# Four integer adds of a weight conversion on GpSimd instead of VectorE, with new tables for the order of block 0, the middle and the stores

## The chip, the cores and the metric

The kernel runs on one core of a Trainium2 chip. Its engines work side by side, each through its own list of instructions in order, and wait for one another by semaphores: TensorE (PE; its weight loads are listed as PEld), VectorE (DVE), ScalarE (ACT), GpSimd (POOL), and SyncE (SP), which here issues the DMA transfers. The metric is the device time of one launch in microseconds (us).

## The reference

Attention in chunks of 64 tokens, and on its output a feed-forward layer with a gate. Cut to what is computed:

```python
batch, n_heads, seq, head_dim = 8, 8, 576, 64              # float32
chunk = 64; scale = 1.0 / np.sqrt(64)
scores = scale * np.matmul(q_c, k_c.transpose(0, 1, 2, 4, 3))   # per chunk of 64
scores = scores - np.max(scores, axis=-1, keepdims=True)
attn = np.exp(scores)
attn = attn / (np.sum(attn, axis=-1, keepdims=True) + 1e-09)
out = np.matmul(attn, v_c)
x = out.transpose(0, 2, 1, 3).reshape(4608, 512)
h = x @ w_in                    # 512 x 2048
g = h * np.clip(h + 3.0, 0.0, 6.0) / 6.0
return g @ w_out                # 2048 x 512
```

## The kernel before

The 4608 tokens are worked on in 9 blocks of 512. A block goes through attention (two parts of four heads each), a first product with w_in, the gate, and a second product with w_out. An fp32 product is made of three matmuls of 128x512 in a shorter format: high by high (L364), high by low (L365), low by high (L366). So every operand has a high half, cast by ScalarE, and a low half, the rest, subtracted by VectorE.

Block 0 is done in plain form, and while it runs the weights are brought in. They come as 64-bit words and are converted tile by tile; tile ft (0 to 15) holds 128 columns of w_in and 128 rows of w_out. Tiles 0 to 3 are converted in halves i (w_in) and o (w_out). The order is written out by hand in the table FIRST, one token for a step, a letter and the tile:

- W load (L152), H high words (ScalarE, L161), L low words (ScalarE, L165), P shift (VectorE, L168), A add of the low bits (VectorE, L171), C cast to the high half (ScalarE, L179), D the low half (VectorE, L187), U store of the converted words (L182, L184), X store of a quarter of the tile for later use (L421). H, P and A work on a scratch tile u, L on a scratch tile r (uh and rh for halves).
- M the first product of block 0 with a tile, N the second; between them the gate: R (ScalarE, L553), G (VectorE, L555), K (ScalarE, L558), B (VectorE, L560).
- A0 and A1 with a small letter or S, Q, V, T: attention of block 1, its two parts. Q and V load; S scores (TensorE, L240); m, u, e, z, x softmax (VectorE, but e on ScalarE); t swap, c place; v multiply (TensorE, L330), h copy of its result (ScalarE, L351), l its low half (VectorE, L352).
- S0, T0 and so on without A: attention of block 0. I: matmuls that fill time.

The tokens are recorded in this order; so on every engine the instructions stand in the order of the tokens that use it, an engine that has to wait holds all that stands behind it, and SP's transfers are issued in token order too. The M and N products use two banks of PSUM called h in turn, and the multiply of block 1's attention uses these two as well: its results are out of them when L352 has run.

Behind block 0 comes the middle (first products of blocks 1 and 2), and then three pairs of blocks, which are done with seven products instead of eight. Their weights are sums of quarters. prepare() makes them: a load of words or an add on VectorE, four adds on GpSimd (L454), a cast on ScalarE (L457), a low half on VectorE (L460), a store to DRAM (L463). The sums and the kept quarters are read back as streams into tiles ws. Tables give the due times, counted in products: MID for the attention of later blocks in the middle, OUT_SUMS and IN_SUMS for the sums, STORES for quarters that are kept in the middle. In the pairs, L481 and L482 make the high and low halves of the operands.

Of the kernel before, what the change touches and what calls it, by code (L numbers as in the profile page):

```python
# [52 lines left out]
FIRST = """
Q0 S0a S0b I0 T0 m0a m0b Q1 W0i u0a u0b S01 I2 S10 I1 m01 e00 u01 z00 e01 S11 I1 T1 m10 H0i W1i V0 z01 W2i L0i m11 x00 W0o x01 L1i W4 P0i n10 I1 e10 z10 V1 H1i
W1o A0i n11 e11 z11 t00 t01 I2 W3i c00 v00 c01 A0Q x10 L2i L0o W5 v01 I2 h00 C0i h01 x11 t10 t11 I0 P1i c10 A1i C1i D0i c11 M0.00 H4 M0.02 H0o l00 l01 M1.00 v10
v11 M1.01 D1i M1.02 M0.01 P4 P0o H2i P2i A2i h10 h11 M1.10 M1.12 A0o l10 l11 L4 M0.12 C0o W3o M0.10 M0.11 M1.11 A4 C2i L1o R0 A0S D2i G0 M2 D0o C4 H3i P3i L3i
D4 K0 B0 N0 A3i A0T H5 W8 R1 G1 H1o C3i K1 D3i M3 P1o P5 A1o L5 B1 R2 G2 L3o C1o W6 D1o H6 M4 A5 P6 R3 G3 U4 C5 D5 W2o K2 B2 L6 N1 H2o L2o H3o M5 A6 P2o W9 A2o
P3o R4 W12 C2o G4 D2o K3 B3 A0m A3o L8 K4 C6 U5 R5 W7 D6 U6 H7 P7 C3o D3o L7 B4 A1Q G5 H8 N2 M6 A7 C7 R6 X4o N3 W13 P8 W10 K5 A8 D7 G6 B5 N4 C8 A0u U7 U8 D8 W11
L9 K6 H10 A0e B6 M7 P10 N5 H9 R7 A0z L10 P9 A0V W14 G7 A9 C9 A0x U9 N6 L11 M8 A0t D9 A10 K7 A0c0 A0c1 A0c2 M9 C10 B7 D10 R8 N7 G8 R9 G9 A0c3 K8 K9 B9 U10 X10o
H11 B8 A1T P11 H12 M10 R10 A11 P12 A0c4 C11 N8 G10 W15 A0v D11 A1S L12 U11 X11i A0h K10 N8e A0l A12 M11 A2Q N9 C12 L13 D12 R11 U12 X8o B10 X0i N10 H13 M12 A1m  # L60
P13 G11 A13 L14 C13 A1u X7i A1e K11 D13 R12 A1z A1x H14 P14 X12i M13 R13 B11 A1V G12 A1t G13 X1o N11 A1c U13 K12 A14 B12 C14 X3o X2o K13 D14 H15 N11e X0o A1v
A1h U14 P15 X5i A1l L15 X5o A15 N12 B13 M14 N13 C15 R14 G14 D15 K14 M15 R15 X3i X7o B14 G15 X14i U15 A2S K15 B15 X13o X15o
""".split()
# [907 lines left out]
```

## Time and profile before

| | us |
|---|---|
| median of 3 runs (lowest, highest) | 774.25 (774.15, 775.13) |
| the profiled execution | 774.06 |
| its span in the trace | 772.2 |
| TensorE busy | 765.9 |
| TensorE weight loads busy | 631.0 |
| VectorE busy | 620.7 |
| ScalarE busy | 409.2 |
| GpSimd busy | 149.4 |

The span is what the trace covers; the time of the execution has 1.86 us around it. TensorE ran at the full clock in all but the last slice of the page's table. Busy times of engines overlap, so they don't add up to the span; what counts is the time in which TensorE waits, and for whom.

### The profile page before, as it was taken

Reading aid. Unit: us, or ns where it says so; the run is one execution under the profiler, and the core shown is the slowest. Engines: PE = TensorE matmul, PEld = TensorE weight load, DVE = VectorE, ACT = ScalarE, POOL = GpSimd, SP = SyncE. Lnnn points to the kernel's source line nnn. Section 1 sums busy time; section 2 is a strip of 40 time slices with the busy share of each in tenths; the row PEclk is TensorE's granted clock in tenths of the full one; section 3 lists DMA queues with packets and bytes.
Section 4 is the critical chain, followed back from the end, with each engine's and each line's share of the span. In section 5 each row is a group of like instructions: output and inputs, shape, how many; then the busy total and the mean of one; then the engine's idle time right before and its main releaser. Section 6 shows DMA issues by size and latency. Waiting matters only on the chain.

```text
span 772.2 us, 13644 instructions
## 1 busy us (share of the span) xinstructions
PE 765.9 (99%) x5551; PEld 631.0 (82%) x5551; DVE 620.7 (80%) x749; ACT 409.2 (53%) x551; POOL 149.4 (19%) x134
## 2 busy tenths in 40 slices
PE   8999999999999999999999999999999999999998
PEld 6788888888888788888888888888888888888887
DVE  6998867888799888787899876778998756669960
ACT  5998646465664534545666434354837333346330
POOL 0000012465561143322300002221100012221000
PEclk9999999999999999999999999999999999999999
DMA  9996898898877798975676777666656775565573
GB/s 363 408 344 234 300 331 306 305 329 293 320 246 248 287 325 300 338 269 187 243 273 238 246 218 256 236 213 223 232 198 219 225 221 191 197 207 200 194 238 113
DMA packets 51838, 199.07 MB, mean 258 GB/s; under 512 B 4672, under 2 KB 10816, under 8 KB 38720
## 3 DMA queue, kind: packets, MB, share of 16 engines
q1 hardware_dynamic: 51488, 197.94, 72.9%
q8 instruction: 44, 0.72, 0.4%
q10 hardware_dynamic: 288, 0.26, 0.1%
q14 instruction: 18, 0.15, 0.1%
HBM read 153.62 MB, written 44.56 MB: 257 GB/s over the span
## 4 chain that ended last, share of the span: by engine, by line
PE 93%; DMA 3%; DVE 2%; ACT 1%; issue 1%; POOL 0%; SPq 0%; ACTq 0%; DVEq 0%; POOLq 0%
PE acc L364 23%; PE acc L365 22%; PE acc L366 22%; PE h L364 7%; PE h L366 7%; PE h L365 7%; PE h L330 2%; PE two L235 2%; DMA a<-hl 1%; DMA hl<-words 1%; PE two L240 1%; DMA qk<-qk_in 1%; POOL hl L454 0%; PE two L309 0%; DVE xop L482 0%
## 5 line engine op out<-in xcount | busy, mean ns | idle before, releaser
L364 PE MATMUL acc<-xop,ws 128*128 128x512 f32 (+1 forms) x616 | 239.6, 389 | 0.0
L365 PE MATMUL acc<-xop,ws 128*128 128x512 f32 (+1 forms) x616 | 239.0, 388 | 0.6 <-DVE xop L482 0.6
L366 PE MATMUL acc<-xop,ws 128*128 128x512 f32 (+1 forms) x616 | 238.8, 388 | 0.0
L365 PEld LDWEIGHTS acc<-xop,ws 128*128 128x128 f32 x616 | 115.7, 188 | 24.6 <-DVE xop L482 1.0
L364 PEld LDWEIGHTS acc<-xop,ws 128*128 128x128 f32 x616 | 115.6, 188 | 23.9
L366 PEld LDWEIGHTS acc<-xop,ws 128*128 128x128 f32 x616 | 115.7, 188 | 23.7
L482 DVE TENSOR_TENSOR xop<-g,xop 128x1024 fp32r<-128x1024 f32 x96 | 117.6, 1257 | 6.8 <-ACT xop L481 6.8
L481 ACT CAST xop<-g 128x1024 fp32r<-128x1024 f32 x96 | 96.9, 1052 | 31.7 <-PE acc L366 22.4
L664 ACT ACTIVATE r<-acc,half 128x512 f32<-128x512 f32 x100 | 66.9, 686 | 68.6 <-DVE acc L631 54.6
L665 DVE SCALAR_TENSOR_TENSOR g<-r,acc 128x512 f32<-128x512 f32 x100 | 66.7, 681 | 41.9 <-ACT r L664 39.2
L454 POOL TENSOR_TENSOR hl<-hl 128x256 f32<-128x256 f32 x64 | 58.4, 915 | 208.5 <-DVE hl L440 111.9
L750 POOL TENSOR_TENSOR g<-g 128x512 f32<-128x512 f32 x24 | 31.0, 1293 | 325.6 <-DVE g L665 325.6
L364 PE MATMUL h<-xop,ws 128*128 128x512 f32 (+1 forms) x176 | 67.8, 385 | 0.0
L366 PE MATMUL h<-xop,ws 128*128 128x512 f32 (+1 forms) x176 | 67.6, 384 | 0.0
L365 PE MATMUL h<-xop,ws 128*128 128x512 f32 (+1 forms) x176 | 67.6, 384 | 0.0
L664 ACT ACTIVATE r<-h,half 128x512 f32<-128x512 f32 x28 | 19.3, 689 | 85.4 <-DVE h L631 83.3
L631 DVE TENSOR_TENSOR u<-h,p 128x512 f32<-128x512 f32 x32 | 22.1, 689 | 32.2 <-PE h L366 25.4
L364 PE MATMUL acc<-x,w 128*128 128x512 f32 x112 | 44.2, 395 | 0.0
L366 PE MATMUL acc<-x,w 128*128 128x512 f32 x112 | 43.6, 390 | 0.0
L365 PE MATMUL acc<-x,w 128*128 128x512 f32 x112 | 43.6, 390 | 0.0
L263 ACT ACTIVATE e<-e 128x1024 f32<-128x1024 f32 (+1 forms) x18 | 18.2, 1013 | 47.8 <-DVE e L261 47.8
L364 PEld LDWEIGHTS h<-xop,ws 128*128 128x128 f32 x176 | 33.1, 188 | 6.6
(120 smaller groups left out, 1217.3 us busy)
## 6 DMA issues: line engine op xcount, KB each, us to landing
ws<-b SPq DMA_DIRECT2D x56, 1024.0 KB, 4.9
ws<-a SPq DMA_DIRECT2D x24, 1024.0 KB, 5.3
ws<-a SPq DMA_DIRECT2D x24, 768.0 KB, 4.4
qk<-qk_in SPq DMA_DIRECT2D x16, 1024.0 KB, 7.7
w<-w_in_out SPq DMA_DIRECT2D x12, 1024.0 KB, 11.6
v<-v_in SPq DMA_DIRECT2D x17, 512.0 KB, 5.9
out_t<-o SPq DMA_DIRECT2D x30, 256.0 KB, 5.9
b<-hl SPq DMA_DIRECT2D x12, 512.0 KB, 5.4
```

Source lines behind the costliest of these rows:

```text
L235: PE.matmul(t[to, a, g, :], lhsT=self.qk[rows, i, 0, c, o], rhs=self.qk[rows, i, 1, c, o], start=True, stop=True)
L263: ACT.activation(out=flat(self.e), in_=src if self.by_product else flat(self.e), func=AF.Exp, scale=SCALE)
L364: PE.matmul(ps, lhsT=a_h, rhs=b_h, start=first, stop=False, skip_group_check=more)
L365: PE.matmul(ps, lhsT=a_h, rhs=b_l, start=False, stop=False, skip_group_check=more)
L366: PE.matmul(ps, lhsT=a_l, rhs=b_h, start=False, stop=last, skip_group_check=more)
L454: POOL.tensor_tensor(out=to, in0=x, in1=y, op=op)
L481: ACT.copy(out=t[:, :, 0], in_=src)
L482: DVE.tensor_tensor(out=t[:, :, 1], in0=src, in1=t[:, :, 0].bitcast(F32), op=ALU.subtract)
L631: return lambda: DVE.tensor_tensor(out=out, in0=x, in1=y, op=ALU.add)
L664: return (lambda: ACT.activation(out=r, in_=ps, func=AF.Relu, bias=half, scale=1.0 / 6.0), lambda: DVE.scalar_tensor_tensor(out=out, in0=r ...
L665: lambda: DVE.scalar_tensor_tensor(out=out, in0=r, scalar=1.0, in1=ps, op0=ALU.min, op1=ALU.mult))
L750: sub = lambda o, x, y: lambda: POOL.tensor_tensor(out=o, in0=x, in1=y, op=ALU.subtract)
```

## The change

The add of the low bits to the converted words goes to GpSimd for four tiles: the whole tiles 15, 6 and 7, and the first half of tile 2. On VectorE it is an instruction of uint16 operands (listed as L171, 128x2048, or 128x1024 for a half); on GpSimd it is an add of int32 words (128x1024, or 128x512). Beside that five tables have new numbers or a new order: FIRST, MID, OUT_SUMS, STORES and IN_SUMS. Tokens that move in FIRST are, among others: A0Q (a load of 1 MB) ahead of W3i; D2i ahead of A0S; A5 ahead of C1o and D1o; X4i (a store) ahead of the loads W9, W12 and W7; U6 behind A1Q; L9 three ScalarE steps later; A0v (multiply) behind A1S (scores); A0V, a load, later. Some stores of quarters go from the middle into FIRST, and STORES has 12 entries for 14.

```diff
-W1o A0i n11 e11 z11 t00 t01 I2 W3i c00 v00 c01 A0Q x10 L2i L0o W5 v01 I2 h00 C0i h01 x11 t10 t11 I0 P1i c10 A1i C1i D0i c11 M0.00 H4 M0.02 H0o l00 l01 M1.00 v10
+W1o A0i n11 e11 z11 t00 t01 A0Q I2 W3i c00 v00 c01 x10 L2i L0o W5 v01 I2 h00 C0i h01 x11 t10 t11 I0 P1i c10 A1i C1i D0i c11 M0.00 H4 M0.02 H0o l00 l01 M1.00 v10
...
-D4 K0 B0 N0 A3i A0T H5 W8 R1 G1 H1o C3i K1 D3i M3 P1o P5 A1o L5 B1 R2 G2 L3o C1o W6 D1o H6 M4 A5 P6 R3 G3 U4 C5 D5 W2o K2 B2 L6 N1 H2o L2o H3o M5 A6 P2o W9 A2o
+D4 K0 B0 N0 A3i A0T H5 W8 R1 G1 H1o C3i K1 D3i M3 P1o P5 A1o L5 B1 R2 G2 L3o A5 C1o W6 D1o H6 P6 M4 R3 G3 U4 C5 W2o K2 X4i D5 B2 L6 N1 H2o L2o H3o M5 A6 P2o W9
...
-STORES = (('X4i', -120), ('X6i', -120), ('X12o', -118.7), ('X9i', -117.2), ('X9o', -113.7), ('X10i', -112), ('X11o', -101.5), ('X8i', -101.3), ('X6o', -99.8), ('X15i', -99), ('X14o', -96.8), ('X13i', -93.1), ('X1i', -89.0), ('X2i', -89))
+STORES = (('X12o', -118.7), ('X10i', -116), ('X11i', -114.7), ('X4o', -112.5), ('X11o', -104.5), ('X9o', -101.7), ('X15i', -99), ('X13i', -93.1), ('X2i', -91), ('X6o', -89.8), ('X1i', -88), ('X14i', -70.4))
+ADDED = ((15, None), (2, 0), (6, None), (7, None))
...
         def add(self):
-            DVE.tensor_tensor(out=self.u, in0=self.u, in1=self.r, op=ALU.add)
+            (POOL if (self.ft, self.m) in ADDED else DVE).tensor_tensor(out=self.u, in0=self.u, in1=self.r, op=ALU.add)
```

Lines of the changed kernel are higher by one from L67 on. GpSimd's list, from its first instructions to the sums of the middle (hl are sums, g operands of a pair), before:

```order
masks.py:199 ISA
masks.py:199 AFFINE_SELECT ident<-ident 128x128
L454 TENSOR_TENSOR hl<-hl 128x256 x20
L685 TENSOR_TENSOR g<-g 128x512 x5
L454 TENSOR_TENSOR hl<-hl 128x256 x4
L685 TENSOR_TENSOR g<-g 128x512
L454 TENSOR_TENSOR hl<-hl 128x256 x4
L685 TENSOR_TENSOR g<-g 128x512 x2
```

and now:

```order
masks.py:199 ISA
masks.py:199 AFFINE_SELECT ident<-ident 128x128
L172 TENSOR_TENSOR uh<-uh,rh 128x512
L172 TENSOR_TENSOR u<-u,r 128x1024 x3
L455 TENSOR_TENSOR hl<-hl 128x256 x20
L686 TENSOR_TENSOR g<-g 128x512 x4
L455 TENSOR_TENSOR hl<-hl 128x256 x4
L686 TENSOR_TENSOR g<-g 128x512 x2
```

The four adds stand first, ahead of all sums; behind them sums and operand adds change places a little.

VectorE's list in block 0, from the conversions of tiles 1 and 5 to those of 2o, 3o and 6 (an ISA row with u or uh is the add; w_1_615 and w_641 are the tiles 1o and 5; w_1_692 is 2o), before:

```order
L187 TENSOR_TENSOR w_1_615<-uh,w_1_615 128x2x256
L171 ISA u<-u,r 128x2048
L168 TENSOR_SCALAR u<-u 128x1024
L555 SCALAR_TENSOR_TENSOR r<-r,h 128x512
L187 TENSOR_TENSOR w_641<-u,w_641 128x4x256
L560 TENSOR_TENSOR g<-r,g 128x512
L171 ISA u<-u,r 128x2048
L168 TENSOR_SCALAR uh<-uh 128x512
L171 ISA uh<-uh,rh 128x1024
L168 TENSOR_SCALAR uh<-uh 128x512
L555 SCALAR_TENSOR_TENSOR r<-r,h 128x512
L187 TENSOR_TENSOR w_1_692<-uh,w_1_692 128x2x256
```

and now (w_1_616, w_641, w_1_691 are the same tiles):

```order
L172 ISA u<-u,r 128x2048
L188 TENSOR_TENSOR w_1_616<-uh,w_1_616 128x2x256
L169 TENSOR_SCALAR u<-u 128x1024
L556 SCALAR_TENSOR_TENSOR r<-r,h 128x512
L188 TENSOR_TENSOR w_641<-u,w_641 128x4x256
L561 TENSOR_TENSOR g<-r,g 128x512
L169 TENSOR_SCALAR uh<-uh 128x512
L172 ISA uh<-uh,rh 128x1024
L169 TENSOR_SCALAR uh<-uh 128x512
L556 SCALAR_TENSOR_TENSOR r<-r,h 128x512
L188 TENSOR_TENSOR w_1_691<-uh,w_1_691 128x2x256
```

The add of tile 5 (first ISA row) stands ahead of the low half of tile 1o, and the add of tile 6, which stood behind the row L560 ahead of the shift of 2o, is gone from this engine.

TensorE's list where tile 11 follows tile 10 (h<-x are first products, acc<-g second ones; w_794 is tile 8, w_963 tile 11), before:

```order
L366 MATMUL acc<-g,w_794 128x512
L330 MATMUL h<-e,v 64x64 x32
L240 MATMUL two<-qk 64x64 x32
L364 MATMUL acc<-g,w_794 128x512
L365 MATMUL acc<-g,w_794 128x512
L366 MATMUL acc<-g,w_794 128x512
L364 MATMUL h<-x,w_963 128x512
L365 MATMUL h<-x,w_963 128x512
```

and now (w_793, w_966):

```order
L367 MATMUL acc<-g,w_793 128x512
L241 MATMUL two<-qk 64x64 x32
L331 MATMUL h<-e,v 64x64 x32
L365 MATMUL acc<-g,w_793 128x512
L366 MATMUL acc<-g,w_793 128x512
L367 MATMUL acc<-g,w_793 128x512
L365 MATMUL h<-x,w_966 128x512
L366 MATMUL h<-x,w_966 128x512
```

The multiply (L330, now L331) and the scores (L240, now L241) have changed places; the rest of TensorE's list is the same from end to end.

## Rows read from the trace of the kernel before

**Rows 1.** The page, part 1: busy time, share of the span, instructions

```profile
PE 765.9 (99%) x5551; PEld 631.0 (82%) x5551; DVE 620.7 (80%) x749; ACT 409.2 (53%) x551; POOL 149.4 (19%) x134
```

**Rows 2.** TensorE's waits: line <- releaser: us in total, times, longest

```profile
PE acc L365 <- DVE xop L482: 0.6, 1, 0.6
PE h L364 <- DVE r L555: 0.3, 1, 0.3
```

**Rows 3.** Timeline of TensorE: start us, us, engine, line, operation, out<-in, count

```profile
46.72 0.39 PE L364 MATMUL h<-x,w 128*128 128x512 f32 x1
46.94 0.39 PE L365 MATMUL h<-x,w 128*128 128x512 f32 x1
47.29 0.50 PE L366 MATMUL h<-x,w 128*128 128x512 f32 x1
...
66.47 0.40 PE L366 MATMUL h<-x,w 128*128 128x512 f32 x1
...
77.30 1.11 PE L240 MATMUL two<-qk 64*64 64x64 f32 x64
78.34 0.50 PE L364 MATMUL acc<-g,w 128*128 128x512 f32 x1
...
79.23 0.50 PE L364 MATMUL h<-x,w 128*128 128x512 f32 x1
```

**Rows 4.** Timeline of VectorE, 39 to 66 us

```profile
39.24 0.68 DVE L560 TENSOR_TENSOR g<-r,g 128x512 fp32r<-128x512 f32 x1
39.84 1.22 DVE L171 CUSTOM_DVE_ANT_0 u<-u,r 128x2048 uint16<-128x2048 uint16 x1
40.98 0.42 DVE L168 TENSOR_SCALAR uh<-uh 128x512 int32<-128x512 int32 x1
41.53 0.69 DVE L171 CUSTOM_DVE_ANT_0 uh<-uh,rh 128x1024 uint16<-128x1024 uint16 x1
...
46.02 1.22 DVE L187 TENSOR_TENSOR w<-u,w 128x1024 fp32r<-128x1024 f32 x1
...
48.77 0.68 DVE L560 TENSOR_TENSOR g<-r,g 128x512 fp32r<-128x512 f32 x1
...
51.11 0.68 DVE L168 TENSOR_SCALAR u<-u 128x1024 int32<-128x1024 int32 x1
...
65.09 1.20 DVE L187 TENSOR_TENSOR w<-u,w 128x1024 fp32r<-128x1024 f32 x1
```

**Rows 5.** Windows, 41.5 to 66.3: us; PE, PEld, DVE, ACT, POOL busy (instructions); clock; DMA

```profile
41.50:66.30 24.80, 24.80 (x110) 20.19 (x108) 24.30 (x32) 21.11 (x26) 0.00 (x0) 1.00 0.81 299
```

**Rows 6.** The page, part 5: GpSimd's adds of L750: busy us, mean ns

```profile
L750 POOL TENSOR_TENSOR g<-g 128x512 f32<-128x512 f32 x24 | 31.0, 1293 | 325.6 <-DVE g L665 325.6
```

**Rows 7.** Timeline of GpSimd

```profile
154.96 2.55 POOL L685 TENSOR_TENSOR g<-g 128x512 f32<-128x512 f32 x2 [1.81 <-DVE g L665]
...
255.21 3.19 POOL L454 TENSOR_TENSOR hl<-hl 128x256 f32<-128x256 f32 x4 [19.55 <-DMA hl<-words]
...
277.26 4.44 POOL L454 TENSOR_TENSOR hl<-hl 128x256 f32<-128x256 f32 x1 [18.87 <-DMA hl<-words]
...
545.37 2.15 POOL L750 TENSOR_TENSOR t<-g 128x512 f32<-128x512 f32 x1
```

**Rows 8.** Timeline of VectorE beside two of those adds

```profile
156.82 0.71 DVE L269 TENSOR_SCALAR z<-z 128x16 f32<-128x16 f32 x1
...
545.03 1.35 DVE L482 TENSOR_TENSOR xop<-g,xop 128x1024 fp32r<-128x1024 f32 x1 [0.24 <-ACT xop L481]
```

**Rows 9.** Line 269: duration ns least/median/longest, first and last start

```profile
L269 DVE TENSOR_SCALAR z<-z x18: 174/175/714, 11.2 to 573.9; 128x16 f32<-128x16 f32 x18
```

**Rows 10.** Timeline of ScalarE

```profile
46.41 1.12 ACT L161 ACTIVATE u<-w 128x1024 f32<-128x1024 f32 x1
...
77.87 1.07 ACT L351 CAST x<-h 128x512 fp32r<-128x512 f32 x2
```

**Rows 11.** DMA issues at 37 to 38 us: count, KB each, us to landing

```profile
w<-w_in_out SPq DMA_DIRECT2D x1, 1024.0 KB, 6.4
```

More of the change, by code (lines that the diff above doesn't have):

```diff
@@ L54 @@
 Q0 S0a S0b I0 T0 m0a m0b Q1 W0i u0a u0b S01 I2 S10 I1 m01 e00 u01 z00 e01 S11 I1 T1 m10 H0i W1i V0 z01 W2i L0i m11 x00 W0o x01 L1i W4 P0i n10 I1 e10 z10 V1 H1i
-W1o A0i n11 e11 z11 t00 t01 I2 W3i c00 v00 c01 A0Q x10 L2i L0o W5 v01 I2 h00 C0i h01 x11 t10 t11 I0 P1i c10 A1i C1i D0i c11 M0.00 H4 M0.02 H0o l00 l01 M1.00 v10
-v11 M1.01 D1i M1.02 M0.01 P4 P0o H2i P2i A2i h10 h11 M1.10 M1.12 A0o l10 l11 L4 M0.12 C0o W3o M0.10 M0.11 M1.11 A4 C2i L1o R0 A0S D2i G0 M2 D0o C4 H3i P3i L3i
-D4 K0 B0 N0 A3i A0T H5 W8 R1 G1 H1o C3i K1 D3i M3 P1o P5 A1o L5 B1 R2 G2 L3o C1o W6 D1o H6 M4 A5 P6 R3 G3 U4 C5 D5 W2o K2 B2 L6 N1 H2o L2o H3o M5 A6 P2o W9 A2o
@@ L58 @@
[L58 to L61, printed above, removed]
@@ L62 @@
-A1h U14 P15 X5i A1l L15 X5o A15 N12 B13 M14 N13 C15 R14 G14 D15 K14 M15 R15 X3i X7o B14 G15 X14i U15 A2S K15 B15 X13o X15o
+W1o A0i n11 e11 z11 t00 t01 A0Q I2 W3i c00 v00 c01 x10 L2i L0o W5 v01 I2 h00 C0i h01 x11 t10 t11 I0 P1i c10 A1i C1i D0i c11 M0.00 H4 M0.02 H0o l00 l01 M1.00 v10
+v11 M1.01 D1i M1.02 M0.01 P4 P0o H2i P2i A2i h10 h11 M1.10 M1.12 A0o l10 l11 L4 M0.12 C0o W3o M0.10 M0.11 M1.11 A4 C2i L1o R0 D2i A0S G0 M2 D0o C4 H3i P3i L3i
+D4 K0 B0 N0 A3i A0T H5 W8 R1 G1 H1o C3i K1 D3i M3 P1o P5 A1o L5 B1 R2 G2 L3o A5 C1o W6 D1o H6 P6 M4 R3 G3 U4 C5 W2o K2 X4i D5 B2 L6 N1 H2o L2o H3o M5 A6 P2o W9
@@ new lines @@
+A2o P3o R4 C2o G4 D2o K3 B3 A0m A3o W12 U5 L8 K4 C6 R5 W7 D6 H7 P7 C3o D3o B4 A1Q U6 G5 L7 H8 N2 M6 A7 C7 N3 R6 P8 W13 W10 K5 A8 D7 G6 N4 C8 B5 A0u U7 D8 U8 W11
+K6 H10 B6 M7 P10 A0e H9 N5 R7 A0z L10 P9 W14 G7 L9 A9 C9 A0x A0V N6 A0t L11 M8 D9 X9i A0c0 R8 U9 K7 A10 A0c1 X6i A0c2 M9 C10 B7 D10 N7 G8 R9 X8i G9 A0c3 K8 K9
+B9 U10 H11 B8 A0c4 H12 P11 X10o M10 R10 A11 A1T P12 C11 N8 G10 A1S D11 W15 L12 A0v A0h N8e A0l A12 U11 K10 M11 H13 A1m N9 C12 R11 A2Q B10 N10 X0i D12 M12 P13
+L13 X7i G11 U12 A13 A1u C13 A1e D13 R12 A1z H14 A1x P14 K11 X12i L14 M13 B11 G12 R13 A1t X8o G13 X1o K12 N11 A1c U13 A14 X3o L15 B12 C14 A1V X2o K13 U14 D14 H15
@@ L63 @@
+N11e A1v A1h P15 X5i A15 A1l N12 B13 M14 N13 X5o C15 R14 G14 D15 K14 M15 R15 X7o G15 B14 A2S U15 K15 X13o B15 X14o X15o X3i X0o
 """.split()
-MID = ((None, -2, -1.0, -1.0, 1.35, 1.35, 1.75, 1.95, (2.1, 2.65, 3.45, 3.75, 4.3), 5.2), (0.5, 4.5, 5.2, 6.15, 6.65, 6.9, 7.65, 9.35, (), 9.5), (5.3, 11.9, 9.8, 10.05, 12.55, 12.55, 12.8, 13.8, (14.5, 14.8, 14.85, 15.15, 15.7), 16.1), (9.9, 18.25, 16.15, 16.5, 17.35, 17.4, 17.55, 17.8, (19.25, 19.3, 20.1, 20.65, 21.2), 21.6), (18.9, 21.05, 21.6, 22.55, 23.15, 23.15, 24.15, 25.05, (25.5, 25.8, 26.1, 26.4, 26.45), 27.2), (23.0, 28.4, 27.45, 27.45, 28.25, 28.25, 28.9, 29.1, (29.55, 29.6, 29.9, 30.2, 31.0), 32.2), (31.75, 32.25, 36.55, 44.05, 44.05, 45.3, 49.0, None, (), None))
@@ L65 @@
-OUT_SUMS = ((0, ('A1',), (-124.6, -124.6, -122.6, -115.7, -114.5, -114.0)), (1, ('L1',), (-114.6, -114.6, -110.7, -107.2, -107.2, -107.2)), (2, ('w0_1', 'w1_1'), (-114.5, -112.0, -112.0, -109.6, -109.1, -108.1)), (3, ('w0_1', 'w1_1'), (-106.0, -103.6, -100.6, -100.6, -100.1, -99.6)), (4, ('w2_1', 'w3_1'), (-105.6, -103.1, -99.6, -93.7, -91.7, -90.0)), (6, ('w0_1', 'w1_1'), (-94.7, -91.7, -89.7, -86.5, -86.5, -80.9)), (7, ('w2_1', 'w3_1'), (-88.5, -87.08, -86.44, -81.9, -81.9, -78.7)), (5, ('w0_1', 'w1_1'), (-80.8, -80.8, -80.8, -75.3, -75.3, -75.3)))
+MID = ((None, -2, -1.0, -1.0, 1.35, 1.35, 1.75, 1.95, (2.1, 2.65, 3.2, 3.5, 3.8), 5.2), (0.5, 4.5, 5.2, 5.9, 7.65, 7.65, 7.65, 9.35, (), 9.5), (5.3, 12.65, 9.8, 10.05, 11.55, 11.55, 12.3, 13.55, (14.25, 14.55, 14.6, 14.65, 15.2), 16.1), (9.9, 19.25, 16.15, 16.75, 17.35, 17.4, 17.55, 17.55, (19.25, 19.3, 19.6, 20.65, 21.2), 21.6), (17.4, 21.55, 21.6, 22.55, 23.15, 23.15, 24.15, 25.05, (25.75, 25.8, 26.1, 26.4, 26.45), 27.2), (23.0, 28.4, 27.2, 27.2, 28.25, 28.25, 28.9, 29.1, (29.55, 29.6, 29.9, 30.2, 31.0), 32.45), (27.75, 33.5, 36.8, 44.3, 44.3, 45.55, 49.0, None, (), None))
@@ new lines @@
+OUT_SUMS = ((0, ('A1',), (-124.6, -124.6, -122.6, -115.7, -114.5, -114.0)), (1, ('L1',), (-114.6, -114.6, -108.7, -107.2, -107.2, -107.2)), (2, ('w0_1', 'w1_1'), (-114.5, -114.0, -114.0, -109.6, -109.1, -108.1)), (3, ('w0_1', 'w1_1'), (-106.0, -103.6, -100.6, -99.6, -99.1, -98.6)), (4, ('w2_1', 'w3_1'), (-105.6, -102.1, -99.1, -94.2, -94.2, -92.2)), (6, ('w0_1', 'w1_1'), (-93.7, -91.2, -90.7, -87.5, -87.5, -84.9)), (7, ('w2_1', 'w3_1'), (-87.5, -87.08, -86.94, -82.9, -79.4, -79.2)), (5, ('w0_1', 'w1_1'), (-80.8, -80.3, -78.8, -75.3, -75.3, -75.3)))
@@ L69 @@
+ADDED = ((15, None), (2, 0), (6, None), (7, None))
 TURNED = ((0, 0), (0, 1), (1, 1), (2, 1))
-IN_SUMS = ((0, ('w0_1', 'w1_1'), (-71.5, -67.0, -63.3, -58.3, -56.0)), (1, ('w2_1', 'w3_1'), (-75.0, -72.0, -64.8, -64.8, -61.0)), (2, ('w2_1', 'w3_1'), (-54.5, -54.5, -43.8, -36.8, -35.8)), (3, ('x1',), (-54.0, -50.0, -42.8, -42.8, -38.8)), (4, ('x1',), (-36.5, -33.5, -30.3, -24.3, -21.3)), (5, ('x1',), (-21.0, -11.0, -7.5, -7.5, -7.5)), (6, ('x1',), (-4.0, 4.0, 7.2, 8.2, 10.0)), (7, ('x1',), (15.0, 21.0, 24.2, 25.2, 27.0)))
+IN_SUMS = ((0, ('w0_1', 'w1_1'), (-73.5, -67.0, -63.3, -58.8, -56.5)), (1, ('w2_1', 'w3_1'), (-75.0, -69.5, -64.8, -64.8, -59.0)), (2, ('w2_1', 'w3_1'), (-54.5, -51.5, -42.8, -35.8, -35.8)), (3, ('x1',), (-57.0, -46.0, -43.8, -43.8, -39.3)), (4, ('x1',), (-36.5, -33.5, -31.3, -28.3, -25.3)), (5, ('x1',), (-21.0, -11.5, -7.5, -7.5, -7.5)), (6, ('x1',), (-4.0, 4.0, 7.2, 8.2, 10.0)), (7, ('x1',), (15.0, 21.0, 24.2, 25.2, 27.0)))
```

## The prediction

> **What bounds the kernel now.** I read the page first, for the engine that has no room left: TensorE is busy for 765.9 us of a span of 772.2, and GpSimd, which gets the new work, for 149.4 [rows 1]. Moving adds and stores can't shorten the products themselves, so only TensorE's waits can be won, or added to. The second view is the list of TensorE's waits: 0.3 us for VectorE's gate (L555), early in block 0, and 0.6 us for VectorE's L482, at the first pair of blocks [rows 2]. The reader is to see how little that is. A wait that the pipeline half hides isn't in that list; it shows in the timeline as a longer step between two matmuls: 0.35 us from 46.94 to 47.29, where the step before (from 46.72) is 0.22 [rows 3], so 0.13 lost. With a handful of that size in block 0, up to 106 us, TensorE's waits after the first matmuls come to some 1.5 us (0.3 + 0.6 + about five of 0.13). 0.2% of the time, what a measurement of this kernel can tell from no change, is 1.55 us. A gain that can be told would need nearly every wait to go.
>
> The other side has no such lid: in block 0 VectorE and TensorE run almost level. VectorE's low half of tile 6 (L187, 46.02 to 47.24) ends just before its matmul at 47.29, that of tile 9 (65.09 to 66.29) 0.18 us before its matmul at 66.47 [rows 3, 4]. Between them VectorE is busy for 24.30 of 24.80 us [rows 5]. Whatever makes it later here reaches TensorE in full.
>
> **GpSimd's price.** No row shows an int32 add on GpSimd. Its f32 add of 128x512 takes 1.29 us [rows 6], and four of 128x256 take 3.19 [rows 7], so 0.80 each. 256 columns more cost 0.49; 128x1024 is 1.29 + 2 x 0.49 = 2.27 us, an estimate from these two rows. VectorE's add of such a tile takes 1.22 (L171) [rows 4]. I take 2.27, the nearest kind of add; the ends are 1.22 (integers as quick as on VectorE) and 3.2 (four times the 0.80, no saving in the longer instruction).
>
> **What it does to VectorE.** GpSimd's 128x512 add issued at 545.37 takes 2.15 instead of 1.29. VectorE's L482 runs from 545.03 to 546.38, and from there it is 1.14 to the add's end [rows 7, 8]: GpSimd did its work after VectorE's instruction, not beside it. It is so the other way round as well. A tensor_scalar of 128x16 takes 0.18 us in the middle of its 18 instances, and 0.71 at the longest [rows 9]: that is the one at 156.82, issued while GpSimd was at two adds (154.96 to 157.51) [rows 7, 8], and it ends 0.02 after them. The steps next to the moved adds are of these kinds: tensor_scalar shifts (L168), and adds and subtractions with both operands in SBUF (L171, L187, L560). L555 and L352 have one operand in PSUM, and I count them as free.
>
> The Trainium skill has this as a rule that speaks against the change ("SBUF — State Buffer", section "Who interferes with whom"): a VectorE instruction with two SBUF inputs, or in a two-port mode, and a GpSimd instruction that reads SBUF exclude each other for the whole instruction, and whoever issues first goes first. The trace agrees, with the 2.15 and the 0.71 above. By the rule the sum is the forecast below; without it, it would be the first rival.
>
> **Part by part.**
> *Tile 2, first half.* VectorE's order was this add, another, two L352, tile 4's add. Now the other add goes first, GpSimd works beside the L352s, and the gate that TensorE waits for 0.3 us can come earlier by as much. That is lost again at 47.29, which hangs on VectorE's chain for tile 6 and not on when TensorE began: 0 (down to -0.3 where that wait goes too).
>
> *Tile 6.* VectorE's L560 ends at 39.92. Then came tile 6's add (39.84, 1.22), the shift of 2o (40.98, 0.42), and 2o's add at 41.53 [rows 4]. Now GpSimd's add and that shift share the time from 39.92 on, in whichever order: 39.92 + 2.27 + 0.42 = 42.61, and only then can the add of 2o start, 1.1 us later than it did. From there to the low half of tile 6 VectorE has no room [rows 5]; ScalarE's cast of tile 6 stands behind that of 2o and moves as much. So the matmul at 47.29 comes at 48.4: +1.1. Ends: -0.1, if nothing is blocked (the 0.35 becomes 0.23), and +2.0 by 3.2 us.
>
> *Tile 7.* VectorE's L560 at 48.77 is followed by a gate with its operand in PSUM, tile 7's add, and the shift of tile 8 at 51.11 [rows 4]. All of it 1.1 later, L560 ends at 50.56, GpSimd works from there to 52.83, and the shift follows at 52.83 instead of 52.21: +0.6. VectorE can't make that up before tile 9's low half [rows 5]. TensorE, itself 1.1 late, has the 0.18 in front of 66.47: +0.4 (0 to +1.4, by 1.22 and 3.2 us).
>
> *Tile 15.* On GpSimd it runs beside two L352, and VectorE's next steps wait for ScalarE in any case: 0 (0 to +0.5).
>
> *The multiply of block 1 (L330) behind A1's scores (L240).* The scores take TensorE from 77.30 to 78.34 [rows 3]; less some 0.1 for the first step of the matmul behind them, the multiply ends 0.95 later, at about 78.4. ScalarE's copy of its result started at 77.87 [rows 10], behind other work; now it starts at 78.45. From its start to the matmul that needs the bank (through L352 on VectorE) were 79.23 - 77.87 = 1.36 us: 79.8 instead of 79.23, +0.55. Ends: 0, if ScalarE is the later one there anyway, and +0.95, if its other work moves as well.
>
> *Reads and stores on SP.* A store of 512 KB, half of a tile's load, now stands ahead of the loads of tiles 9, 12 and 7. Tile 7's, issued at 37.33, landed 6.4 us later at 43.7 [rows 11]; ScalarE takes it up at 46.41 [rows 10]. Half of 6.4, with all its queueing, would be 3.2, against a cover of 2.7, and ScalarE's 1.1 from above makes it 3.8. So 0; if the cover were gone, up to +0.5. The other moved loads and stores have no less.
>
> *Middle and sums.* VectorE's low halves of sums (L460) and some adds change places with their neighbours, one or two places at 0.7 to 1.2 us each, with TensorE not waiting there now. The wait of 0.6 [rows 2] hangs on one chain: a sum's store, the load behind it, four GpSimd adds at 255.21 [rows 7], a cast on ScalarE, L481, L482. Each engine still takes these in the same order: 0 (-0.6, where the transfers of that chain find more room, to +0.5).
>
> Sum: 1.1 + 0.4 + 0.55 = 2.1 us onto the profiled execution, whose own time is 774.06 (its span of 772.2 and 1.86 around it): 776.2. The median of the runs, 774.25, is 0.2 above that execution, less than any term; I leave it at 776.2. This case's own range is 775.2 to 777.2.
>
> **Rivals.**
> *The adds hide.* GpSimd's int32 add is about as quick as VectorE's, or stands less in its way than the rows say. Then VectorE gains room, the waits of block 0 up to 66 us shrink (-0.2), and only the multiply costs: 774.06 - 0.2 + 0.55 = 774.4, no change. For it: no row of such an add, and GpSimd idle all through block 0. Against it: the 2.15 and the 0.71.
> *Faster.* VectorE, rid of four adds (0.7 + 3 x 1.22 = 4.4 us), gets far enough ahead that all waits of block 0 go (0.9), the multiply's is covered too, and the new order of sums takes the 0.6 away: 774.06 - 1.5 = 772.6. It decides from the shift of 2o: that has to start before 40.98. Against it: the chain behind the 0.6 has nothing of block 0 in it.
> *GpSimd starved.* At 277.26 a 128x256 add took 4.44 us instead of 0.80 [rows 7], 3.6 more. If tile 7's add fares so between VectorE's instructions, its cast and low half are 3.6 later still, of which about 3 reach TensorE: 779. Against it: the gate with its PSUM operand stands right there.
>
> **How the numbers follow.** Forecast 0.57, adds hidden 0.27, faster 0.06, starved 0.10. Within 0.2% (772.70 to 775.80) are the hidden case, about a fifth of the forecast's weight (its range begins at 775.2) and a little of the third: 0.40. Slower than that: 0.55. Faster: 0.05. The range of 773.9 to 777.3 leaves out the starved case, the faster one, and the outer ends of the others.
>
> **What would show it.** On GpSimd one add of 1.3 us or more near 23 us, and three of 2.3 or more near 40, 50 and 100. On VectorE over 1 us more, as a gap or a long instruction, between the L560 at 39 and the add of 2o, and 0.6 behind the L560 at 49. On TensorE the L366 of tile 6's product about 1.1 later behind a long step, 0.4 more at tile 9's, 0.55 more in front of tile 11's, and the 0.6 for L482 as before. It is wrong if the shifts and adds beside GpSimd's keep 0.42 and 0.69, or if the matmul of 47.29 stands where it stood.

## The result, and the profile after

| | kernel before | changed kernel |
|---|---|---|
| median of the runs, us | 774.36 (6 runs) | 777.90 (6 runs) |
| ratio, 95% interval | | 1.0051 (1.0034 to 1.0068) |
| the same, measured again | 774.19 (30 runs) | 777.64 (7 runs); 1.0042 (1.0024 to 1.0059) |
| the profiled execution, span | 774.06, 772.2 | 779.97, 777.8 |

Slower by 0.4 to 0.5%, some 3.3 to 3.9 us. The forecast was 776.2, slower, with a range up to 777.3: the direction is right, the size is not. A part of the difference lies outside the traces: an execution of the changed kernel takes 2.2 to 2.3 us more than its span, in each of its 13 runs, and one of the kernel before 1.8 to 2.0, in each of the 30. These 0.4 us are in no table below, and their cause stays open (the kernel before with the new tables alone, e6_new_tables, has 2.1 to 2.2).

The page of the changed kernel and its list of TensorE's waits (us in total, times, longest), against [rows 1, 2]:

```profile
PE 768.7 (99%) x5551; PEld 631.7 (81%) x5551; DVE 622.7 (80%) x745; ACT 409.7 (53%) x551; POOL 160.3 (21%) x138
```

```profile
PE two L241 <- DMA x<-qk_in: 2.0, 1, 2.0
PE h L367 <- DVE w L188: 0.7, 2, 0.4
PE h L365 <- DVE x L353: 0.5, 1, 0.5
PE h L331 <- ACT e L296: 0.4, 1, 0.4
```

The first of these waits is at 8 us, before anything that the change moved, and is not in the second profile of the changed kernel in this size (0.7). So I don't compare spans. I take the start of the same matmul in both traces, and count from 28 us on. An example: the matmul at 47.29 [rows 3] is at 50.72 below; the first product that began at 27.54 before, behind the wait for the gate, begins at 29.88; 3.43 less 2.34 is 1.09 us lost between them. TensorE of the kernel before at that start:

```profile
27.54 0.50 PE L364 MATMUL h<-x,w 128*128 128x512 f32 x1 [0.27 <-DVE r L555]
```

and of the changed kernel, at that start and at the three places of the forecast:

```profile
29.88 0.50 PE L365 MATMUL h<-x,w 128*128 128x512 f32 x1
...
49.89 0.39 PE L366 MATMUL h<-x,w 128*128 128x512 f32 x1
50.72 0.50 PE L367 MATMUL h<-x,w 128*128 128x512 f32 x1 [0.44 <-DVE w L188]
...
70.27 0.50 PE L367 MATMUL h<-x,w 128*128 128x512 f32 x1 [0.21 <-DVE w L188]
...
82.95 0.39 PE L367 MATMUL acc<-g,w 128*128 128x512 f32 x1
83.85 0.50 PE L365 MATMUL h<-x,w 128*128 128x512 f32 x1 [0.52 <-DVE x L353]
```

The same subtraction for every profile gives this table (us lost in each stage against the first profile of the kernel before, negative: won; stages by that profile's time; the names are those of the experiments):

| profile | 28-50, tile 6 | 50-72, tile 9 | 72-82, tile 11 | 82-104, tile 14 | 104-259, middle | 259-270 |
|---|---|---|---|---|---|---|
| changed | 1.09 | 0.57 | 0.62 | 0.09 | 1.76 | -0.89 |
| changed, second (r2_after) | 1.10 | 0.56 | 0.63 | 0.05 | 2.00 | -0.90 |
| before, second (r1_before) | -0.02 | 0.03 | 0.03 | 0.02 | 0.08 | -0.90 |
| e1_adds_on_dve | 0.12 | 0.17 | 0.62 | 1.35 | 1.45 | -0.89 |
| e11_tile15_back | -0.04 | 0.17 | 0.60 | 0.06 | 1.38 | -0.89 |
| e2_before_67 | 1.39 | 0.47 | 0.03 | -0.01 | -0.01 | -0.89 |
| e10_67_cast_later | 1.12 | 0.44 | 0.01 | 0.02 | 0.47 | -0.43 |
| e3_multiply_first | 1.08 | 0.57 | 0.38 | 0.09 | 0.94 | -0.90 |
| e12_repaired | 0.23 | 0.17 | 0.41 | 0.03 | 1.07 | -0.89 |
| e5_stores_behind | 1.13 | 0.53 | 0.59 | 0.06 | 0.93 | -0.90 |
| e6_new_tables | 0.11 | -0.02 | 0.03 | 0.02 | 0.87 | -0.89 |
| e4_old_middle | 1.13 | 0.51 | 0.63 | 0.06 | 3.33 | -0.89 |
| e9_cast_later | 0.31 | -0.01 | 0.02 | 0.02 | 1.37 | -0.89 |

How far such a number can be trusted shows in profiles with the same order: e9_cast_later has the order of the kernel before up to 255 us and still loses 0.31 in the first column and 1.37 in the middle; e1_adds_on_dve and e11_tile15_back have the same order up to tile 14 and differ by 0.16 in the first.

Now the engines behind these steps. VectorE of the changed kernel, the place of [rows 4]:

```profile
41.83 0.69 DVE L561 TENSOR_TENSOR g<-r,g 128x512 fp32r<-128x512 f32 x1
42.43 0.42 DVE L169 TENSOR_SCALAR uh<-uh 128x512 int32<-128x512 int32 x1
42.99 2.67 DVE L172 CUSTOM_DVE_ANT_0 uh<-uh,rh 128x1024 uint16<-128x1024 uint16 x1
...
53.60 2.11 DVE L169 TENSOR_SCALAR u<-u 128x1024 int32<-128x1024 int32 x1
```

GpSimd's four adds:

```profile
25.41 1.68 POOL L172 TENSOR_TENSOR uh<-uh,rh 128x512 int32<-128x512 int32 x1 [24.10 <-DVE uh L169]
41.84 3.27 POOL L172 TENSOR_TENSOR u<-u,r 128x1024 int32<-128x1024 int32 x1 [14.75 <-ACT r L166]
52.61 2.54 POOL L172 TENSOR_TENSOR u<-u,r 128x1024 int32<-128x1024 int32 x1 [7.50 <-ACT r L166]
104.75 2.40 POOL L172 TENSOR_TENSOR u<-u,r 128x1024 int32<-128x1024 int32 x1 [49.59 <-DMA a<-w]
```

GpSimd issued tile 6's add at 41.84 and VectorE kept the way through two instructions, until 42.43 + 0.42 = 42.85; from there GpSimd ran 2.26 us, to 45.11 (the forecast took 2.27). VectorE's add of 2o, issued at 42.99, ends at 45.66, 0.55 after that: it needs 0.69 and took 2.67. The shift of tile 8 needs 0.68 and took 2.11. ScalarE's cast of 2o, and behind it all of its list, waits for that add (before, 0.36 us at the same place):

```profile
45.70 0.62 ACT L180 CAST w<-uh 128x512 fp32r<-128x512 f32 x1 [1.67 <-DVE uh L172]
```

In the middle one VectorE instruction waits longer in the changed kernel than in the one before: a gate that needs the landing of a store of words. VectorE and SP of the changed kernel:

```profile
134.40 1.28 DVE L666 SCALAR_TENSOR_TENSOR g<-r,h 128x512 f32<-128x512 f32 x2 [2.55 <-DMA words<-u]
```

```profile
125.94 1.01 SPq L397 DMA_DIRECT2D out_t<-g  x2
127.00 0.94 SPq L422 DMA_DIRECT2D a<-w  x2
128.03 0.40 SPq L679 DMA_DIRECT2D words<-u  x1
```

and the same of the second profile of the kernel before:

```profile
127.42 0.69 DVE L665 SCALAR_TENSOR_TENSOR g<-r,h 128x512 f32<-128x512 f32 x1 [1.18 <-DMA words<-u]
```

```profile
119.50 2.37 SPq L396 DMA_DIRECT2D out_t<-g  x4
121.97 0.40 SPq L678 DMA_DIRECT2D words<-u  x1
```

The reader is to see the two stores a<-w, which are now issued right ahead of the store that the gate waits for.

The last column of the table was a surprise: the wait of 0.6 near 261 us [rows 2] is in the first profile of the kernel before and, but for a rest in one, in none of the thirteen others, its own second profile among them.

### The profile page after: what moved, and what is told of

Same layout as the page of the kernel before. It is cut to its first block, busy times and chain, and to the rows that moved or that the text cites. A ratio compares the mean times of both kernels' runs of the same rounds, so it can differ in the third digit from the quotient of the medians.

```text
span 777.8 us, 13650 instructions
## 1 busy us (share of the span) xinstructions
PE 768.7 (99%) x5551; PEld 631.7 (81%) x5551; DVE 622.7 (80%) x745; ACT 409.7 (53%) x551; POOL 160.3 (21%) x138
## 4 chain that ended last, share of the span: by engine, by line
PE 82%; DVE 7%; ACT 5%; DMA 3%; issue 1%; SPq 0%; DVEq 0%; ACTq 0%
PE acc L365 20%; PE acc L367 20%; PE acc L366 20%; PE h L365 6%; PE h L367 6%; PE h L366 6%; PE h L331 2%; DMA b<-hl 2%; PE two L236 1%; DVE hl L461 1%; DMA x<-qk_in 1%; ACT w L180 1%; ACT r L166 1%; DVE w L188 1%; DVE e L273 1%
## 5 line engine op out<-in xcount | busy, mean ns | idle before, releaser
L666 DVE SCALAR_TENSOR_TENSOR g<-r,acc 128x512 f32<-128x512 f32 x100 | 66.8, 681 | 44.1 <-ACT r L665 41.5
L482 ACT CAST xop<-x 128x1024 fp32r<-128x1024 f32 x21 | 21.8, 1053 | 32.0 <-DVE x L498 18.4
```

The lines of the kernel that those rows point to most:

```text
L482: ACT.copy(out=t[:, :, 0], in_=src)
L666: lambda: DVE.scalar_tensor_tensor(out=out, in0=r, scalar=1.0, in1=ps, op0=ALU.min, op1=ALU.mult))
```

## The experiments

**All adds on VectorE (e1_adds_on_dve).**

```diff
-ADDED = ((15, None), (2, 0), (6, None), (7, None))
+ADDED = ()
```

> The changed kernel with all adds on VectorE again, the new order and tables kept. Theory of the port (GpSimd and VectorE exclude each other): the 1.1 us lost at the products of tiles 2 and 6 (44 to 47 us of the kernel before) and the 0.5 at tile 9 go; TensorE keeps the 0.7 in front of tile 11 and what the middle costs. Against the kernel before some 1.0 to 1.8 less loss than the changed kernel has: 775.8 to 776.8 where that has 777.9. Theory of the order (the new order of block 0 and of its reads costs it, the adds are free): nothing changes, 777.5 to 778.3, and the steps at 47 and 66 stay. Theory of the middle (all that counts is lost in the middle, block 0 is taken back): also about 777.9, with the steps of block 0 gone.

Measured: 776.91, ratio to before 1.0026 (1.0014 to 1.0039). At tile 6 the loss is 0.12 for 1.09, at tile 9 0.17 for 0.57: the port's theory is right on both, 0.97 and 0.40, though the time is a little above its 775.8 to 776.8. What no theory had: 1.35 us in front of tile 14's product. Its bank is freed by L353, and in the new order tile 15's add stands ahead of that on VectorE. TensorE and VectorE of this kernel:

```profile
102.12 0.50 PE L365 MATMUL h<-x,w 128*128 128x512 f32 x1 [1.16 <-DVE x L353]
```

```profile
100.23 1.23 DVE L172 CUSTOM_DVE_ANT_0 u<-u,r 128x2048 uint16<-128x2048 uint16 x1
101.38 1.28 DVE L353 TENSOR_TENSOR x<-h,x 128x512 fp32r<-128x512 f32 x2
```

So in the new order the four adds on GpSimd cost TensorE 1.37 at tiles 6 and 9 and save 1.26 at tile 14. By themselves they come out even in block 0.

**The same with tile 15's add behind L353 (e11_tile15_back).**

```diff
-X5i A15 A1l N12
+X5i A1l A15 N12
```

> The new order and tables, all adds on VectorE, and tile 15's add again behind the low halves (L352) of block 1's attention, where the kernel before has it. Theory of the place (the 1.3 us in front of tile 14's product, at 100 us, came from that add standing ahead of the L352 which frees the bank): it goes, under 0.1 is left, and 775.6 to 776.2. Theory that ScalarE or the moved loads cause it: 1.3 stay, 776.9. By either, nothing is lost at 47 and 66 us.

Measured: 776.08, ratio 1.0020 (1.0004 to 1.0035). The 1.35 is gone (0.06), by the place theory. VectorE and TensorE:

```profile
100.09 1.28 DVE L353 TENSOR_TENSOR x<-h,x 128x512 fp32r<-128x512 f32 x2
101.29 1.21 DVE L172 CUSTOM_DVE_ANT_0 u<-u,r 128x2048 uint16<-128x2048 uint16 x1
```

```profile
100.83 0.50 PE L365 MATMUL h<-x,w 128*128 128x512 f32 x1
```

No add is on GpSimd here, and the kernel is still slower than before: what is left is the cost of the new order and tables, 0.17, 0.60 and 1.38 us.

**Tiles 6 and 7 alone on GpSimd (e2_before_67).** In the kernel before:

```diff
+ADDED = ((6, None), (7, None))
-            DVE.tensor_tensor(out=self.u, in0=self.u, in1=self.r, op=ALU.add)
+            (POOL if (self.ft, self.m) in ADDED else DVE).tensor_tensor(out=self.u, in0=self.u, in1=self.r, op=ALU.add)
```

> The kernel before with the adds of tiles 6 and 7 alone on GpSimd, its own order and tables kept. Theory of the port: TensorE loses about 1.1 us at tile 6 and 0.4 to 0.5 at tile 9, nothing in front of tile 11 beyond the 0.1 of before: +1.5 at 70 us, and if that isn't taken back at the wait of 0.6 near 261, 775.6 to 776.0. Theory of the order: less than 0.3 at 70 us, 774.2 to 774.6. If later waits take it back: +1.5 at 70 us and +0.6 to +0.9 at the end, 775.0 to 775.3.

Measured: 775.37, ratio 1.0013 (1.0003 to 1.0023). TensorE loses 1.39 and 0.47. The rows are those of the changed kernel again, only that here VectorE leaves a gap of 0.31 behind the row L561, GpSimd comes first, and the shift is the one that is blocked, 2.24 instead of 0.42:

```profile
40.22 2.47 POOL L172 TENSOR_TENSOR u<-u,r 128x1024 int32<-128x1024 int32 x1 [38.92 <-ACT r L166]
```

```profile
40.73 2.24 DVE L169 TENSOR_SCALAR uh<-uh 128x512 int32<-128x512 int32 x1 [0.31 <-ACT uh L162]
43.11 0.69 DVE L172 CUSTOM_DVE_ANT_0 uh<-uh,rh 128x1024 uint16<-128x1024 uint16 x1
```

```profile
48.87 0.50 PE L367 MATMUL h<-x,w 128*128 128x512 f32 x1 [0.47 <-DVE w L188]
```

The end was only 1.0 later than before, and I took it that the wait near 261 gives up to 0.87 back. The next two runs were to test that.

**The cast of sum 4 later, in the kernel before (e9_cast_later) and with tiles 6 and 7 on GpSimd (e10_67_cast_later).**

```diff
-(4, ('x1',), (-36.5, -33.5, -30.3, -24.3, -21.3))
+(4, ('x1',), (-36.5, -33.5, -28.3, -24.3, -21.3))
```

> The kernel before with one number of IN_SUMS changed: the cast (L457) of sum 4 due at -28.3 instead of -30.3, so that on ScalarE one L481 stands ahead of it. Theory of the in-order wait (the 0.9 us near 261 is that L481, ready long before, behind a cast that waits for a transfer): the wait of 0.6 goes, TensorE issues without a break, 0.75 to 0.9 less than before: 773.3 to 773.6. Theory that L481 or L482 itself is late: no change, 774.4.

> The kernel before with the adds of tiles 6 and 7 on GpSimd and the cast of sum 4 later as well. Theory that the wait near 261 takes back up to 0.87 us of what was lost ahead of it: without that wait nothing is taken back, all of the 1.8 to 1.9 us of block 0 reaches the end: 1.8 to 2.0 above the kernel with the cast later alone, so about 775.3, where the adds alone cost 1.0 against the kernel before. If the loss is taken back elsewhere: 1.0 above it.

Measured: 774.39, ratio 1.0004 (0.9994 to 1.0015), and 775.54, 1.0025 (1.0010 to 1.0040). The first gains nothing, where the wait's theory had 0.8. The other theory's 774.4 is met, but by luck: the wait is gone in this profile (-0.89), and 1.7 were lost elsewhere. The second is 1.1 above the first, as the adds alone were above the kernel before: by the number, the wait doesn't take their loss back. The reason came with the repeat below: the wait that I meant to remove isn't there in the other profiles either. The first kernel shows another thing. Its order up to 255 us is that of the kernel before, and yet it lost 1.37 in the middle. GpSimd and VectorE there, near 172 to 178 us:

```profile
172.44 3.74 POOL L454 TENSOR_TENSOR hl<-hl 128x256 f32<-128x256 f32 x4 [1.91 <-DMA hl<-words_out]
```

```profile
175.71 0.50 DVE L269 TENSOR_SCALAR z<-z 128x16 f32<-128x16 f32 x1
...
176.53 1.98 DVE L272 TENSOR_TENSOR e<-e,z 128x1024 f32<-128x1024 f32 x1
```

and VectorE in the second profile of the kernel before:

```profile
174.05 0.18 DVE L269 TENSOR_SCALAR z<-z 128x16 f32<-128x16 f32 x1
...
174.54 1.44 DVE L272 TENSOR_TENSOR e<-e,z 128x1024 f32<-128x1024 f32 x1
```

GpSimd's adds here start when a transfer lands. Which VectorE instructions they then meet differs from one execution to the next; in this one two of them take 0.3 and 0.5 us longer. What decides it no run shows.

**The multiply ahead of the scores again (e3_multiply_first).**

```diff
-C11 N8 G10 A1S D11 W15 L12 A0v A0h N8e
+C11 N8 G10 A0v D11 A1S W15 L12 A0h N8e
```

> The changed kernel with the multiply of block 1's attention again ahead of the scores, where the kernel before has it; all else as changed. Theory of the port and the loop (multiply, copy, low half, bank free): the step of 0.7 in front of tile 11 shrinks to 0.1, at 80 us 0.6 less than the changed kernel; at the end 0.6 less (777.3), or none if the wait near 261 takes it. Theory that ScalarE or a load is the later one there: no difference at 80 us.

Measured: 777.49, ratio 1.0032 (1.0015 to 1.0048). A miss by both theories: of the 0.62, 0.24 goes. The loop of multiply, copy and low half is short again, and tile 11's product follows without a wait, but the multiply itself now waits for a gate on VectorE, which empties its other bank:

```profile
77.80 1.09 PE L331 MATMUL h<-e,v 64*64 64x64 f32 x58 [0.26 <-DVE r L556]
...
80.38 0.39 PE L367 MATMUL acc<-g,w 128*128 128x512 f32 x1
80.61 0.40 PE L365 MATMUL h<-x,w 128*128 128x512 f32 x1
```

**The old tables of the middle (e4_old_middle), the two stores behind the store of words (e5_stores_behind), and the new tables in the kernel before (e6_new_tables).** In the first MID, OUT_SUMS and IN_SUMS are those of before; in the second:

```diff
-('X10i', -116), ('X11i', -114.7), ('X4o', -112.5)
+('X4o', -112.5), ('X10i', -112), ('X11i', -111)
```

and the third is the kernel before with the three new tables.

> The changed kernel with the tables MID, OUT_SUMS and IN_SUMS of the kernel before (order of block 0, stores and GpSimd's adds as changed). Theory of the middle: the 1.8 us that TensorE loses between 130 and 216 us are gone (under 0.4 left); at the end, since the wait near 261 then comes back with 0.6 to 0.9, 0.9 to 1.2 less than the changed kernel (776.7 to 777.0). If the lateness of block 0 and the moved stores make the loss in the middle and not the tables: it stays within 0.4, and the time with it.

> The changed kernel with the stores X10i and X11i due at -112 and -111 instead of -116 and -114.7, so that SP issues them behind the store of words (L679) at 128 us. Theory of the store queue (these two stores make that store land later, VectorE's gate waits for it, and VectorE has no room after that): the gate's wait of 2.55 us at 134 shrinks to 0.7 to 1.7, TensorE's 0.2 at 131 (us of the kernel before) is gone and of the 1.8 us between 130 and 216 at least half. At the end not less than 0.9 is left to lose before the wait near 261 comes back: 776.9 to 777.5. Theory of the tables (VectorE's sums stand in the wrong places): only the 0.2 goes, 1.4 to 1.6 stay.

> The kernel before with the changed kernel's MID, OUT_SUMS and IN_SUMS, everything else as before. Theory of the store queue: block 0 as before (under 0.2 difference at 100 us), and between 130 and 216 us at most 0.5 lost; at the end within 0.4 of before. Theory of the tables: 1 to 1.6 lost there, of which the wait near 261 takes back up to 0.9: 774.6 to 775.2.

Measured: 778.74, 1.0047 (1.0031 to 1.0063); 776.56, 1.0043 (1.0028 to 1.0057); 774.77, 1.0010 (0.9995 to 1.0024). The old tables make the middle worse, 3.33 for 1.76, which neither theory had: that the new tables alone cost the 1.8 falls. With the stores behind, 0.93 is left. SP issues the words first now, and VectorE's gate no longer waits for them:

```profile
124.43 0.40 SPq L679 DMA_DIRECT2D words<-u  x1
```

```profile
129.76 1.43 DVE L666 SCALAR_TENSOR_TENSOR g<-r,h 128x512 f32<-128x512 f32 x2 [0.44 <-ACT e L296]
```

And the new tables in the kernel before, with no other change, lose 0.87, between the two expectations, at 183 us, where the multiply waits for ScalarE's copies behind a later transpose, and at 216:

```profile
183.75 0.64 PE L330 MATMUL h<-e,v 64*64 64x64 f32 x28 [0.32 <-ACT e L295]
```

The transpose is later because a step of the softmax ahead of it takes 1.02 us instead of 0.18 and ends with GpSimd's add beside it:

```profile
174.95 1.02 DVE L269 TENSOR_SCALAR z<-z 128x16 f32<-128x16 f32 x1
```

```profile
174.65 1.29 POOL L685 TENSOR_TENSOR g<-g 128x512 f32<-128x512 f32 x1
```

How much of the 1.76 and 2.00 is the stores' can be read over all profiles, since nearly all that TensorE loses in the middle is lost at three places (us lost as above, stretches by the time of the first profile of before):

| stores, tables | profiles | 132-146 | 184-190 | 210-218 |
|---|---|---|---|---|
| ahead of the words, new | changed | 0.68, 0.66 | 0.68, 0.69 | 0.35, 0.62 |
| ahead of the words, new | e1, e11, e3 | 0.48, 0.49, 0.66 | 0.35, 0.25, 0.27 | 0.62, 0.39, 0.01 |
| behind the words, new | e5, e12 | -0.01, -0.01 | 0.67, 0.69 | 0.16, 0.34 |
| as before, new | e6 | -0.01 | 0.65 | 0.19 |
| ahead of the words, old | e4 | 1.22 | 1.19 | 0.88 |
| as before, old | before (second), e2, e10, e9 | -0.01 each | 0.00, 0.00, 0.47, 1.18 | 0.02, 0.01, 0.00, 0.19 |

The first stretch follows the stores without an exception: 0.5 to 0.7 lost with the new tables (1.2 with the old) wherever they stand ahead of the store of words, nothing elsewhere. So 0.7 of the changed kernel's loss is theirs. The other 1.0 to 1.3 are at the two later places. There the new tables lose in every profile, but the old ones lost as much or more in some, with GpSimd's adds beside VectorE's softmax; that the tables cause it isn't shown. The end times can't settle it: the intervals of the second and third kernel don't set them apart from their neighbours.

**The two kernels again (r1_before, r2_after).** Nothing is edited.

> The kernel before, unchanged, profiled a second time. If the loss of 1.8 us between 130 and 216 us belongs to the change, the middle is as in its first profile: under 0.3 difference between 100 and 260 us. If the middle varies from one execution to the next by how GpSimd's and VectorE's instructions meet (the kernel with the cast later, which has the same order up to 255 us, lost 1.4 there), it differs by 0.4 to 1.5, and the wait near 261 is smaller by as much. Time 774.2 in any case.

> The changed kernel, unchanged, profiled a second time. The steps of block 0 are fixed by the order: 1.1 at tile 6, 0.5 at tile 9, 0.6 to 0.7 in front of tile 11, within 0.1. The late load at 8 us of its first profile (2.0 us) is not there. If the middle's 1.8 belongs to the change, 1.6 to 2.0 again; if it varies, 0.5 to 2.5. Time 777.2 to 778.2.

Measured: 773.41, ratio 0.9990 (0.9976 to 1.0003), and 777.64, 1.0042 (1.0024 to 1.0059). The steps of block 0 repeat within 0.04 in these two pairs, the middle within 0.24 for the changed kernel and 0.08 for the one before. The wait near 261 is gone without any lateness ahead of it. TensorE's windows from 258 to 263 us, first the changed kernel, then the second profile of the one before; the first profile of before had 4.40 busy there:

```profile
258.00:263.00 5.00, 5.00 (x24) 4.14 (x23) 4.65 (x7) 1.06 (x1) 2.68 (x4) 1.00 1.01 366
```

```profile
258.00:263.00 5.00, 5.00 (x24) 4.14 (x23) 4.33 (x6) 5.00 (x6) 0.00 (x0) 1.00 0.62 202
```

The chain ahead of it was quicker: its load of words took 7.3 us from issue to landing in the first profile, and in the second 5.9, and the four adds behind it ran at 253.58 instead of 255.21 [rows 7]:

```profile
hl<-words SPq DMA_DIRECT2D x1, 512.0 KB, 7.3
```

```profile
hl<-words SPq DMA_DIRECT2D x1, 512.0 KB, 5.9
```

```profile
253.58 3.20 POOL L454 TENSOR_TENSOR hl<-hl 128x256 f32<-128x256 f32 x4 [18.27 <-DMA hl<-words]
```

Against this repeat the second profile of the changed kernel loses 3.44 + 0.53 = 4.0 us from 28 us to the end (3.44 against the first profile, which the repeat beats by 0.53 over the same stretch). The runs give 3.3 to 3.9, and 0.4 of that is outside the spans; so these two executions are further apart than typical ones (that of the repeat, 773.04, is among the quicker of its kernel).

**Three costs taken out (e12_repaired).** The changed kernel with the edits of e3 and e5, and

```diff
-ADDED = ((15, None), (2, 0), (6, None), (7, None))
+ADDED = ((15, None), (2, 0))
```

> The changed kernel with the three costs taken out that the runs have shown: adds of tiles 6 and 7 on VectorE (those of 15 and of the half of 2 stay on GpSimd), the multiply ahead of the scores, the two stores behind the store of words. If these are all of the loss: block 0 within 0.3 of before at 110 us, the middle within what repeats of the kernel before show, and the time within 0.2% of before, 774.0 to 775.0. If something else of the new order costs: over 0.6 lost by 110 us, or 775.5 and more.

Measured: 775.59, ratio 1.0011 (0.9999 to 1.0022), between the two expectations. By 104 us 0.84 is lost, not under 0.3: 0.41 of it is at the multiply waiting for VectorE's gate, as in e3:

```profile
78.58 1.09 PE L331 MATMUL h<-e,v 64*64 64x64 f32 x58 [0.25 <-DVE r L556]
```

No add of tile 6 or 7 is on GpSimd here, so it isn't these that make the gate late; the new order of block 0 is left for it. The 0.23 of the first column is within what profiles of one order differ by. The middle's 1.07 is at the two later places, with nothing at that of the stores. About half of the change's loss is found and undone by this (1.91 are left at 259 us, of 4.1 and 4.3); no version here beats the kernel before.

## Why the prediction was wrong

*What bounds the kernel.* Right: nothing in the change could win much, and VectorE's lateness in block 0 reached TensorE in full.

*GpSimd's price.* Right: 2.27 taken, 2.26 from the end of the blocking instruction to its own at tile 6, 2.40 at tile 15, where nothing blocked it.

*Tile 6, tile 7, the lock.* Right. Tile 6 was forecast at 1.1 and measured at 1.09 and 1.10, of which 0.97 is the adds' against e1 and 1.13 against e11. Tile 7 was forecast at 0.4, seen at tile 9: 0.57, of which 0.40 is the adds'. Both rivals that change this, the adds hidden and GpSimd starved, are out by the same rows: what the Trainium skill says ("SBUF — State Buffer", "Who interferes with whom") held, with VectorE's 0.69 become 2.67 and GpSimd 2.26 long once it had the way. One thing of it the trace doesn't bear out, that whoever issues first goes first: GpSimd's add was issued at 41.84, and VectorE's shift, issued at 42.43, still went ahead of it.

*Tile 2, tile 15, the reads of block 0.* 0 was forecast for each. Between 28 and 50 us the new order without the adds loses nothing (-0.04 in e11), so the loads of block 0 cost nothing there. Tile 2's add runs before 28 us, where the profiles differ by up to 3 us; no run shows what it costs. Tile 15: 0.09 and 0.05. That hid two things that cancel: the new place of the add would cost 1.3 on VectorE, and GpSimd saves it. The add isn't free for VectorE there either; its L561 takes 1.97 for 0.69, and TensorE loses nothing by it:

```profile
105.73 1.97 DVE L561 TENSOR_TENSOR g<-r,g 128x512 fp32r<-128x512 f32 x1
```

*The multiply.* 0.55 forecast, 0.62 measured, by the loop that was named. That undoing it gives back just 0.24 was not foreseen.

*Reads and stores on SP; middle and sums.* Here it failed. The text gave the moved stores "no less" cover than tile 7's load, and the sums 0, "with TensorE not waiting there now". The middle lost 1.76 and 2.00 us. For the stores the cover was already negative in the trace of before: a VectorE gate waited 1.2 us for the landing of the store of words, and two stores more ahead of it made that 2.55. I had looked at TensorE's waits there, where there were none, and not at those of the engine that feeds it. 0.7 is this. The other 1.0 to 1.3 were lost at 184 to 190 and 210 to 218 us, among the sums and the attention steps of the new tables, which I had seen move and priced at nothing. At the first of these places GpSimd's adds lengthen VectorE's softmax (a step of 0.18 takes 1.02 to 1.04 in e6 and in both profiles of the changed kernel), the very lock that was priced in block 0 and left out here. Whether the new tables are to blame stays open: the first profile of before has 0.63 for that step and loses nothing.

*The wait of 0.6.* It was carried along as part of the kernel (0, down to -0.6). It is in that one execution and not in its repeat. In my sum against the profiled execution it counts as 0.9 won.

*The time outside the span.* The 1.86 was carried over; the changed kernel's is 0.4 more, and no run shows why.

The sum with these sizes: 1.1 + 0.57 + 0.62 + 0.09 + 1.76 - 0.89 = 3.25 from 28 us on, for 2.1. With the 0.4 outside the span it is 3.7, where the runs show 3.3 to 3.9. Against an execution in which that wait isn't there, the 0.89 is not won either, and the sum is above the runs; what typical executions of the kernel before lose instead isn't shown. In the start, before 28 us, the 13 profiles lie between 0.8 ahead of the first profile of before and 2.3 behind it; the changed kernel's two are the latest (2.34 and 1.80), but of the six others with its order of block 0, or nearly so, five are ahead by 0.2 to 0.8 and one is 1.25 behind. Whether the change takes a part there stays open.
